# Values loaded as seven consecutive keys per partition, with the keys in the same order; scalings of q put off and turns of x moved

## The chip, the cores and the metric

The kernel runs on one core of one Trainium2 chip, as one launch. The metric is the device time of the launch in microseconds (us). Before the change three runs gave a median of 1261.9 us (1261.85 to 1263.39).

## The reference

Two blocks stand one after the other, all in float32. The first is attention with normalised queries and keys, for 8 batches of 12 heads, 448 positions and 64 channels; the second is an MLP mixer on the joined heads (768 channels).

```
q_n, k_n = rmsnorm(q, g_q), rmsnorm(k, g_k)             # over the 64 channels
attn = softmax(q_n @ k_n.T / sqrt(64))                  # over 448 keys
x = (attn @ v), heads side by side                      # 8 x 448 x 768
h = relu(x.T @ w_tok1) @ w_tok2                         # 448 -> 256 -> 448
u = x + h.T
out = u + relu(u @ w_ch1) @ w_ch2                       # 768 -> 1536 -> 768
```

The sum over the keys is the same in whatever order the keys are taken, as long as scores and values take the same one. That is what the change uses.

## The kernel before, in words

The work is written for heads in pairs: pair p holds two heads, there are 48 pairs, six to a batch, and two pairs are worked on together. The 448 keys of a head stand in NK = 7 blocks of 64. For each block the PE forms the scores with the keys as the stationary side (L475, into a PSUM tile s_ps), ACT takes their exponentials (L479, tile e), and the PE multiplies them with the values (L560, out to o_ps). The sums over the keys are made by matmuls with ones for the first pairs (L532) and by additions on DVE and POOL with one matmul for the later ones.

**How keys and queries come in.** `loads` (in class Pre, ending in L1625) fetches q and k of a pair. For pairs 0 to 11, called plain, q and k come by rows, and `turn_qk` turns them on the PE (L443, into t_ps); ACT then copies the keys out of PSUM (L453) and copies and scales the queries (L449). For pairs 12 to 47 q and k come in blocks of 32 by 32, four DMAs of 32 partitions for each, and DVE turns them (L446, one instruction for the keys of a pair and one for the queries, 72 in all). There the queries are scaled by ACT in place (L449) in a step of its own, `finish_q`. The scores of a pair wait for it; `score` calls it itself if it has not been called by then.

**How values come in.** `load_v` issues two DMAs for each pair on SP, one for each head (L417). A partition r holds the keys r, 64 + r, 128 + r and so on: seven runs of 64 floats (256 bytes) each. Three buffers (v_0, v_1, v_2, printed as v_69, v_70, v_71) take turns, and a load waits until the PE has used the values that were in its buffer. A SP DMA also waits for the completion of the one eight before it, as there are eight semaphores in rotation.

**The order of the work.** Each engine runs its instructions in the order in which the program issues them. A planner keeps a list of items with a cost in microseconds; `merge` lays lists between each other by these costs, and `later(us, fn)` puts a call off until the items issued since then have cost that much. `att_step(g)` gives the items of attention for the first 18 pairs (four steps to two pairs), `big_step` those of the later ones. Up to pair 19 the scaling is put off with `later(3.0, ...)` at L839.

**Turns of x.** In batch 0 the attention's output (tile uT) has to be turned for the token mixing. `trans_x` does it for 128 channels at a time: four PE transposes (L929, L931, into t_ps, the same PSUM banks as the scores), and three copies by ACT (L933 once, L935 twice). There are six such turns. `x_items(0, 0)` holds the first three and `x_items(0, 1)` the others; tok1 (L953, L960) is the first token matmul, which reads them.

**The first stage.** While batch 0 goes through its channel mixing (L1175 and on), the channel weights are still being converted from their form in DRAM: DMAs of raw (L231), then DVE (L354, L355, L357, L359, L388) and ACT (L365), chunk by chunk, in a chain that the matmuls of L1175 wait for. L1186 is a copy of ACT that frees one of their PSUM tiles. Later batches fetch the converted weights from DRAM (ws) by L1133, as tiles named unit.

Of the kernel before, what the change touches and what calls it, by code (L numbers as in the profile page):

```python
# [83 lines left out]
def whole(ctx, tc, shifted, pre, q, k, v, g_q, g_k, moe_w_tok1, moe_w_tok2, moe_w_ch1, moe_w_ch2, out):  # L84
# [328 lines left out]
    def load_v(p):  # L413
        b, hs = heads(p)
        st["v", p] = vt = pre.v_0 if p == 0 else st["v45"][:, p - 4, :] if p in (4, 5) else pre.v_t[p % 3]
        for a in range(2):
            nc.sync.dma_start(  # L417
                out=vt[rows_of(p, a)].rearrange("r (k d) -> r k d", d=D),
                in_=v[b, hs][a].rearrange("(k r) d -> r k d", r=D))

    def rows_of(p, a):

        return slice((a ^ p % 2) * D, (a ^ p % 2) * D + D)

    def scale(p):
        pre.scale(p, st)
# [6 lines left out]
    def turn_qk(p, i, apart=False):  # L433

        qk = st["qk", p]
        if ("qkT", p) not in st:
            st["qkT", p] = pre.qkT[p] if p < len(pre.qkT) else qkT_pool.tile([P, 2, S], F32, name="qkT")[:]
        to = st["qkT", p][:, i, :]
        if pre.plain(p):
            ps = s_tile("t_ps")  # L440
            for c in range(NS):
                o = (i * NS + c) * P
                nc.tensor.transpose(ps[:, c * R:(c + 1) * R], qk[0:R, o:o + P], ident[0:R, 0:R])  # L443
            src = ps[:, 0:S]
        else:
            nc.vector.transpose(out=to, in_=qk[:, i * S:(i + 1) * S])  # L446
            src = to
        if i == 0:
            st["mul", p] = lambda: nc.scalar.mul(to, src, g_t[:, 0:1])  # L449
            if not apart:  # L450
                finish_q(p)
        elif pre.plain(p):
            nc.scalar.copy(out=to, in_=src)  # L453
        if i == 0:
            st.pop(("qk", p))
# [297 lines left out]
    def att_step(g):  # L753
# [67 lines left out]
        if live and n < NP:  # L821
            late = n < 2 * NPAIR + 2
            if t >= NPAIR // 2 and late:
                if s == 1:
                    ahead, behind = f(pre.square, n), f(pre.reduce, n) + f(pre.square, n + 1)
                elif s == 2:
                    behind = f(pre.reduce, n + 1) + pre.roots(n, st) + scales(n)
                    if pre.plain(n):
                        sooner, behind = behind[:-2], [lambda: None] * len(behind[:-2]) + behind[-2:]
            elif t >= NPAIR // 2:  # L830
                a, b = f(pre.square, n) + f(pre.reduce, n), f(pre.square, n + 1) + f(pre.reduce, n + 1)
                behind = (a, b + pre.roots(n, st), scales(n), [])[s]
            now = {2: [] if pre.plain(n) else [n], 3: [n, n + 1] if pre.plain(n) else [n + 1]}.get(s, [])
            apart = not (shifted or pre.plain(n))

            def turn(q, i):
                turn_qk(q, i, apart)
                if apart and i == 0:
                    later(3.0, lambda: finish_q(q))  # L839
            turns = [lambda q=q, i=i: turn(q, i) for q in now for i in (1, 0)]  # L840

        inside = g < 2 * NPAIR
# [565 lines left out]
    AHEAD = 1  # L1408
# [36 lines left out]
    for part in pre.roots(2, st):  # L1445
        part()
    scale(2)
    scale(3)
    run(merge(
        att_items(1, 8) + merge(att_items(8, AHEAD * per + 1), x_items(0, 0)),  # L1450
        [(0.4, lambda: None)] + weight_items(0, BEFORE)))
    left, (some, sums) = [], sum_items()
    for b in range(B):
        early, double = middle_items(b)
        if b == 0:
            early, last = first_items(
                tok1_items(0, 0) + x_items(0, 1) + tok1_items(0, 1) + early, double, some)
        else:
            if b > 1 and in_next(b - 1):

                y, z = sends(b - 1, y_order(b - 1)[:4]), left
                left = [y[0], y[1], z[0], y[2], z[1], y[3]]
            run(merge(tok1_items(b, 0), left[:2]))
            begin, early = merge(tok1_items(b, 1) + early[:3 * KC], left[2:]), early[3 * KC:]
            if b == 1 and not shifted:
                run(merge(begin, sums[5:9]))
                early, begin = merge(early[:8], sums[9:]) + early[8:], []
            elif b == 1:
                early, begin = merge(begin + early[:8], sums[5:]) + early[8:], []
            if b == 1:  # L1470
                form_items()
            tail, keep = (4, 2) if b == 1 else (14, 3) if ending(b) else (11, 6)
            last, ends = double[-tail - keep:-tail], double[-tail:]
            double = double[:-tail - keep]
            early = begin + early + double
        lo = (b + AHEAD) * per + 1
        att = []
        if b + AHEAD < B and (shifted or b < 2):
            att = att_items(lo, lo + 10) + x_items(b + AHEAD, 0)
            if shifted:  # L1480
                att += att_items(lo + 10, lo + per)
            elif not b:
                step = att_step(lo + per - 1)
                att += att_items(lo + 10, lo + per - 1) + step[:5] + x_items(1, 1) + step[5:]
            else:
                run(att[:6])
                ahead, block, beside, between = big_step(BIG, False)
                att = att[6:] + att_items(lo + 10, lo + per - 1) + ahead + [block] + beside
                att += between[:6] + x_items(2, 1) + between[6:-3]
                behind_x = between[-3:]  # L1490
        elif b + AHEAD < B:
            t = (b + AHEAD) * NPAIR // 2
            blocks = [big_step(t + i // 2, i % 2) for i in range(1, NPAIR + 1)]
            blocks[4][3][10:10] = x_items(b + 1, 0)
            early = place(early, blocks, [near(early, at) for at in BLOCKS], in_seven(b))
        if b == 0:
            last = x_items(1, 1) * shifted + merge(last, sums[:5], turns(b, y_order(b)[2:4]))
        else:
            if b + 1 < B:
                last = merge(last, behind_x if b == 1 and not shifted else x_items(b + 1, 1))  # L1500
            if b == 2 and not shifted:
                last.append((0.4, right_sums))
            last += last_items(b, ends)
        run(merge(att, early) + last)
        if b == 0:
            load_units(0)
        left = [] if b and ending(b) else turns(b, y_order(b)[4:])
# [5 lines left out]
class Start:  # L1513
# [95 lines left out]
    def loads(self, p, st, eng, other):  # L1609
# [13 lines left out]
        def blocks(e, i, x, m):  # L1623
            o = 32 * m % D
            e.dma_start(  # L1625
                out=qk[32 * m:32 * m + 32, i * S:(i + 1) * S].rearrange("t (n c) -> t n c", c=32),
                in_=x[b, hs][32 * m // D][:, o:o + 32].rearrange("(n t) c -> t n c", t=32))

        fn, n = (plain, 2) if self.plain(p) else (blocks, 4)
        return [lambda e=e, i=i, x=x, m=m: fn(e, i, x, m)  # L1630
# [152 lines left out]
```

## Time and profile before

| | |
|---|---|
| median of three runs | 1261.9 us |
| the profiled execution: its time | 1260.77 us |
| the profiled execution: its span | 1259.0 us |
| granted TensorE clock, mean | 0.998 |
| PE busy | 1231.8 us, 98% |
| DVE, POOL, ACT busy | 871.6, 448.9, 418.9 us |

The time of the profiled execution holds 1.8 us that lie outside its span. The profile is one execution as the hardware profiler recorded it. Its page has the busy time of each engine, the span in 40 slices, the DMA queues, the chain of work that ended last, and groups of instructions. The trace behind it can be asked for one engine's instructions in a stretch of time (a timeline: start, length, engine, line, operation, tiles, count, and in brackets the idle time before it with what ended it), for all waits of one engine, for the busy time of every engine in given stretches, and for the time from a DMA's issue to its landing.

### The profile page before, as it was taken

How to read it: one execution, taken by the hardware profiler on the slowest of the kernel's cores; microseconds unless marked ns; L12 is line 12 of the kernel's file. 1: busy time of each engine (PE TensorE's matmuls, PEld its weight loads, DVE VectorE, ACT ScalarE, POOL GpSimd, SP SyncE). 2: the span in 40 equal slices, each digit the busy share in tenths (PEclk: the TensorE clock that was granted, in tenths of full speed). 3: DMA queues.
4: the chain of work that ended last, by engine and by line, in shares of the span. 5: the costliest groups of instructions: out<-in, count | busy, mean ns of one | idle time of the engine just before them, and what ended most of it. 6: DMA issues, size and time to landing. Idle time of an engine off the chain costs nothing.

```text
span 1259.0 us, 21357 instructions
## 1 busy us (share of the span) xinstructions
PE 1231.8 (98%) x7724; PEld 903.2 (72%) x7724; DVE 871.6 (69%) x1385; ACT 418.9 (33%) x896; POOL 448.9 (36%) x681
## 2 busy tenths in 40 slices
PE   6999998999999999999999999999999999999998
PEld 4444443457744488797778877897787877798998
DVE  6888899757774466877688486866768486656243
ACT  5764443224332144302442144312444034301210
POOL 2220650034996831334233232344132342133222
PEclk9999999999999999999999999999999999999999
DMA  8565797999899886794768667694777865487564
GB/s 199 120 169 157 214 256 194 207 250 251 228 246 208 199 203 167 159 244 93 178 166 216 158 152 177 152 238 102 188 169 161 214 129 155 120 201 175 167 175 105
DMA packets 480279, 228.46 MB, mean 181 GB/s; under 512 B 362900, under 2 KB 440084, under 8 KB 480164
## 3 DMA queue, kind: packets, MB, share of 16 engines
q1 hardware_dynamic: 472626, 211.85, 68.9%
q0 software_dynamic: 4512, 14.46, 3.9%
q8 instruction: 63, 1.03, 0.4%
q10 hardware_dynamic: 3026, 0.69, 0.3%
q14 instruction: 52, 0.43, 0.1%
HBM read 184.26 MB, written 42.66 MB: 180 GB/s over the span
## 4 chain that ended last, share of the span: by engine, by line
PE 78%; DVE 6%; DMA 1%; issue 1%; SPq 0%; ACT 0%; DVEq 0%; ACTq 0%
PE m_ps L1205 26%; PE m_ps L1271 22%; PE s_ps L475 8%; PE o_ps L560 8%; PE m_ps L1254 4%; PE t_ps L953 2%; PE m_ps L953 2%; PE seven_ps L1039 2%; PE m_ps L1039 1%; PE m_ps L1085 1%; DVE raw L357 1%; DVE raw L355 1%; PE m_ps L1175 1%; DVE stage L388 1%; DVE es L516 1%
## 5 line engine op out<-in xcount | busy, mean ns | idle before, releaser
L1271 PEld LDWEIGHTS m_ps<-hb,unit 128*128 128x128 f32 x1440 | 271.6, 190 | 7.4 <-issue 3.5
L1271 PE MATMUL m_ps<-hb,unit 128*128 128x224 f32 x1440 | 276.1, 353 | 0.2 <-ACT e L479 0.2
L1205 PE MATMUL m_ps<-tu,unit 128*128 128x224 f32 x1008 | 202.0, 355 | 2.0 <-DVE hb L1211 1.6
L1205 PEld LDWEIGHTS m_ps<-tu,unit 128*128 128x128 f32 x1008 | 189.0, 190 | 16.1 <-issue 7.8
L479 ACT ACTIVATE e<-s_ps 128x448 f32<-128x448 f32 x294 | 138.9, 548 | 122.4 <-PE s_ps L475 120.9
L475 PE MATMUL s_ps<-qkT 64*64 64x448 f32 (+1 forms) x1344 | 152.8, 545 | 1.2 <-ACT x L935 1.1
L1205 PE MATMUL m_ps<-uT,unit 128*128 128x224 f32 x756 | 151.1, 354 | 0.7 <-DVE hb L1211 0.6
L1205 PEld LDWEIGHTS m_ps<-uT,unit 128*128 128x128 f32 x756 | 142.2, 190 | 7.6 <-POOL tu L1109 3.1
L560 PE MATMUL o_ps<-e,v 64*64 64x448 f32 (+1 forms) x1288 | 136.5, 538 | 0.9 <-DMA v<-in_v_dram 0.7
L516 DVE TENSOR_TENSOR es<-es,e 128x896 f32<-128x896 f32 x90 | 101.3, 1126 | 8.7 <-ACT e L479 4.0
L1211 POOL TENSOR_TENSOR hb<-r,r 128x448 f32<-128x448 f32 x21 | 24.0, 1142 | 218.1 <-ACT r L1227 218.1
L475 PEld LDWEIGHTS s_ps<-qkT 64*64 64x64 f32 (+1 forms) x1344 | 46.9, 129 | 72.9 <-issue 51.2
L560 PEld LDWEIGHTS o_ps<-e,v 64*64 64x64 f32 (+1 forms) x1288 | 48.1, 127 | 61.0 <-issue 55.2
L1211 DVE TENSOR_TENSOR hb<-m_ps,r 128x448 f32<-128x448 f32 x63 | 38.9, 618 | 70.1 <-POOL r L1211 49.3
L1690 POOL TENSOR_TENSOR nt<-rs 128x56 f32<-128x56 f32 (+1 forms) x54 | 21.3, 394 | 180.3 <-DVE rs L1682 177.1
L1286 POOL TENSOR_TENSOR uT<-uT,r 128x448 f32<-128x448 f32 x42 | 54.6, 1315 | 77.9 <-DVE r L1286 50.5
L1212 ACT ACTIVATE hb<-hb 128x448 f32<-128x448 f32 x84 | 48.4, 576 | 101.3 <-DVE hb L1211 84.2
L1660 DVE TENSOR_REDUCE ms<-sq 128x28 f32<-128x896 f32 (+2 forms) x44 | 46.9, 1068 | 45.2 <-ACT sq L1647 38.7
L329 POOL TENSOR_TENSOR raw<-raw 128x128 f32<-128x128 f32 x128 | 68.2, 552 | 26.7 <-DMA raw<-wp 22.2
L1175 PE MATMUL m_ps<-hb,stage 128*128 128x448 f32 x144 | 57.4, 556 | 4.9 <-ACT r L1186 3.8
L1282 ACT COPY r<-m_ps 128x448 f32<-128x448 f32 x24 | 12.8, 532 | 140.2 <-PE m_ps L1271 140.2
L1711 DVE TENSOR_TENSOR qk_t<-qk_t,rs 128x896 f32<-128x896 f32 (+1 forms) x42 | 54.7, 1340 | 2.3 <-POOL rs L1693 2.3
(184 smaller groups left out, 1769.2 us busy)
## 6 DMA issues: line engine op xcount, KB each, us to landing
unit<-ws SPq DMA_DIRECT2D x267, 384.0 KB, 4.0
raw<-in_moe_w_ch_dram SPq DMA_DIRECT2D x72, 256.0 KB, 3.8
v<-in_v_dram SPq DMA_DIRECT2D x96, 112.0 KB, 3.9
out_dram<-turned SPq DMA_DIRECT2D x182, 56.0 KB, 2.0
xs<-xt SPq DMA_DIRECT2D x52, 168.0 KB, 4.1
qk_t<-in_q_dram SPq DMA_DIRECT2D x144, 56.0 KB, 3.5
qk_t<-in_k_dram SPq DMA_DIRECT2D x144, 56.0 KB, 3.7
x<-xs SPq DMA_DIRECT2D x39, 192.0 KB, 3.9
```

The lines of the kernel that those rows point to most:

```text
L329: nc.gpsimd.tensor_tensor(out=at[o], in0=at[x], in1=at[y], op=ALU.add if op == "+" else ALU.subtract)
L475: nc.tensor.matmul(out=pss[i][to:to + wide, 0:S], lhsT=qkT[h, 1, k * D + o:k * D + o + wide], rhs=qkT[h, 0, :], start=True, stop=True)
L479: nc.scalar.activation(out=e[:, i, :], in_=pss[i][:, 0:S], func=AF.Exp)
L516: nc.vector.tensor_tensor(out=es[:], in0=(es if k > 1 else st["e", t, 0])[:], in1=st["e", t, k][:], op=ALU.add)
L560: nc.tensor.matmul(out=st["o", p][o:o + wide, 0:S], lhsT=vt[rows, k * D + d:k * D + d + wide], rhs=e[rows, :], **kw)
L953: nc.tensor.matmul(out=st["t1", h][jc][:, 0:HC], lhsT=w1_sb[:, c, jc * P:(jc + 1) * P], rhs=st["x", b, h][:, :, c, :], start=start and c = ...
L1175: nc.tensor.matmul(out=ps, lhsT=a[:, o + 2 * half, :], rhs=natural(half * KF + t) if wide else u[:, half * KC + t, :], start=(t == 0 and h ...
L1205: nc.tensor.matmul(out=ps[:, j * HS:(j + 1) * HS], lhsT=w[:, t, j, :], rhs=m, start=(t == 0), stop=(t == KC - 1))
L1211: add = lambda e, o, x, y: e.tensor_tensor(out=o, in0=x, in1=y, op=ALU.add)
L1271: nc.tensor.matmul(out=ps[:, x * HS:(x + 1) * HS], lhsT=st["w"][:, tile_at % 6, :], rhs=hb[:, X_SLOT[f], i, :], start=(i == 0), stop=(i == 3))
L1286: e.tensor_tensor(out=get(out), in0=get(x_), in1=get(y), op=ALU.add if op == "+" else ALU.subtract)
L1711: self.nc.vector.tensor_tensor(out=part, in0=part, in1=r.unsqueeze(2).to_broadcast(list(part.shape)), op=ALU.mult)
```

## The change

It has four parts.

1. The values of a pair are loaded so that a partition holds seven consecutive keys, one run of 448 floats (1792 bytes). Plain pairs still take two DMAs of 64 partitions. The other pairs take four DMAs of 32 partitions, since there the 64 partitions of a block are two groups of 32 in another order of keys.
2. The keys are put in the same order: for plain pairs by the ACT copy out of PSUM, which now reads every seventh float; for the others by a k load that takes another order of rows, and by a DVE turn whose blocks are read and written in another order. The queries stay as they were.
3. The scaling of q is put off by 8.0 instead of 3.0 in the planner's microseconds. This concerns pairs 12 to 19.
4. Four of the six turns of x in batch 0, not three, lie among the attention steps ahead of its last one; that last step stands by itself behind them. The other two turns follow with the token mixing.

```diff
@@ load_v
         for a in range(2):
-            nc.sync.dma_start(
-                out=vt[rows_of(p, a)].rearrange("r (k d) -> r k d", d=D),
-                in_=v[b, hs][a].rearrange("(k r) d -> r k d", r=D))
+            to, src = vt[rows_of(p, a)], v[b, hs][a]
+            if pre.plain(p):
+                nc.sync.dma_start(out=to, in_=src.rearrange("(r k) d -> r (k d)", r=D))
+                continue
+            src = src.rearrange("(t m k) d -> m t (k d)", m=2, k=NK)
+            for m in range(2):
+                nc.sync.dma_start(out=to[32 * m:32 * m + 32], in_=src[m])
@@ turn_qk
             src = ps[:, 0:S]
+            if i:
+                src = src.rearrange("p (r k) -> p k r", k=NK)
+                to = to.rearrange("p (k r) -> p k r", k=NK)
         else:
-            nc.vector.transpose(out=to, in_=qk[:, i * S:(i + 1) * S])
+            src = qk[:, i * S:(i + 1) * S]
+            if i:
+                nc.vector.transpose(
+                    out=to.rearrange("p (k m c) -> p m k c", m=2, c=32),
+                    in_=src.rearrange("p (m k c) -> p m k c", m=2, c=32))
+            else:
+                nc.vector.transpose(out=to, in_=src)
@@ att_step
-                    later(3.0, lambda: finish_q(q))
+                    later(8.0, lambda: finish_q(q))
@@ the call of the first steps
+    first_x = x_items(0, 0) + x_items(0, 1)
     run(merge(
-        att_items(1, 8) + merge(att_items(8, AHEAD * per + 1), x_items(0, 0)),
+        att_items(1, 8) + merge(att_items(8, AHEAD * per), first_x[:KC + 1]) + att_items(AHEAD * per, AHEAD * per + 1),
         [(0.4, lambda: None)] + weight_items(0, BEFORE)))
...
-                tok1_items(0, 0) + x_items(0, 1) + tok1_items(0, 1) + early, double, some)
+                tok1_items(0, 0) + first_x[KC + 1:] + tok1_items(0, 1) + early, double, some)
@@ blocks, in loads
-                in_=x[b, hs][32 * m // D][:, o:o + 32].rearrange("(n t) c -> t n c", t=32))
+                in_=x[b, hs][32 * m // D][:, o:o + 32].rearrange("(t n) c -> t n c" if i else "(n t) c -> t n c", t=32))
```

The numbers of lines grow by 13 in most of the program (L475 becomes L488, L449 becomes L462, L1186 becomes L1199).

On ACT, at pair 12 (about 194 to 210 us of the trace before), these rows stood one behind the other; L449 is the scaling, L479 the exponentials, L365 a step of the weight conversion, r the copy of L1186:

```order
L449 ACTIVATE qkT<-qkT,g_t 128x448
L479 ACTIVATE e<-s_ps 128x448 x4
L365 ACTIVATE raw<-raw,expo_c 128x512 x2
L1186 COPY r_19297<-m_ps 128x448
L1186 COPY r_19302<-m_ps 128x448
```

In the change the same place reads:

```order
L492 ACTIVATE e<-s_ps 128x448 x4
L365 ACTIVATE raw<-raw,expo_c 128x512
L462 ACTIVATE qkT<-qkT,g_t 128x448
L365 ACTIVATE raw<-raw,expo_c 128x512
L1199 COPY r_19371<-m_ps 128x448
L1199 COPY r_19376<-m_ps 128x448
```

The scaling of pair 12 has moved behind the four exponentials and one conversion step, and stays ahead of the two copies.

On PE, at the end of batch 0's attention (about 70 to 82 us), with t_ps and uT the turns of x, L953 and L960 tok1, L475 the scores:

```order
L475 MATMUL s_ps<-qkT 64x448 x4
L929 MATMUL t_ps<-ident,uT 128x128 x3
L931 MATMUL t_ps<-ident,uT 64x128
L953 MATMUL m_ps<-x,w_sb 128x384 x3
L960 MATMUL m_ps<-x,w_sb 128x384 x2
L475 MATMUL s_ps<-qkT 64x448 x8
```

In the change:

```order
L488 MATMUL s_ps<-qkT 64x448 x4
L966 MATMUL m_ps<-x,w_sb 128x384 x3
L973 MATMUL m_ps<-x,w_sb 128x384 x2
L488 MATMUL s_ps<-qkT 64x448 x8
```

The third turn is gone from the place right ahead of tok1: it stands some 20 rows earlier, and the fourth a few rows behind it, among the scores and values of pairs 4 and 5. Behind the second part of tok1 two turns follow each other where there were three.

On SP, in a batch of the later part (at about 758 us of the trace before), the loads of values for two pairs and the weight tiles beside them:

```order
L1133 DMA unit<-ws_17246 128x768 x5
L417 DMA v_71<-in_v_dram 64x7x64 x2
L417 DMA v_69<-in_v_dram 64x7x64 x2
L1133 DMA unit<-ws_17246 128x768 x2
```

In the change:

```order
L1146 DMA unit<-ws_17318 128x768 x5
L423 DMA v_71<-in_v_dram 32x448 x4
L423 DMA v_69<-in_v_dram 32x448 x4
L1146 DMA unit<-ws_17318 128x768 x2
```

The values of two pairs take eight issues on SP where they took four, and the weight tiles behind them follow four issues later.

## The prediction

> **What bounds the kernel now.** I read the page first, then all waits of PE, then the chain, then timelines at the few places where PE stands still. The page:
>
> ```profile
> PE 1231.8 (98%) x7724; PEld 903.2 (72%) x7724; DVE 871.6 (69%) x1385; ACT 418.9 (33%) x896; POOL 448.9 (36%) x681
> PE 78%; DVE 6%; DMA 1%; issue 1%; SPq 0%; ACT 0%; DVEq 0%; ACTq 0%
> ```
>
> PE is busy for 1231.8 of 1259.0 us, and the chain is PE for 78% of the span. No matmul is removed here; the change can only win what PE loses in waits. All waits of PE:
>
> ```profile
> PE first_ps L163 <- DVE ms L1660: 10.3, 1, 10.3
> PE m_ps L1175 <- ACT r L1186: 3.8, 2, 3.3
> PE m_ps L1205 <- DVE hb L1211: 2.2, 2, 1.6
> PE s_ps L475 <- ACT x L935: 1.1, 2, 0.8
> PE m_ps L953 <- ACT x L933: 0.9, 1, 0.9
> PE s_ps L475 <- ACT e L479: 0.9, 1, 0.9
> ...
> PE o_ps L560 <- DMA v<-in_v_dram: 0.7, 1, 0.7
> ```
>
> Without the start's 10.3 us and the 2.2 us on L1211, which the change doesn't touch, there are 3.8 + 1.1 + 0.9 + 0.9 + 0.7 = 7.4 us for it to win. Whether a wait counts depends on its place, so next the chain between 150 and 272 us (start, length, what):
>
> ```profile
> 223.43 3.35 DMA raw<-in_moe_w_ch_dram
> ...
> 241.47 0.97 DVE ms L1660
> 243.09 9.29 PE m_ps L1175 x24
> ```
>
> From about 161 us to 243.09 the pieces of the chain are nearly all DVE's conversions of the channel weights; ahead of that and from 243.09 on it is PE. So a wait of PE between these two points is worth nothing by itself: PE meets the conversion chain at 243.09 anyway. A wait ahead of it counts, if DVE waits for PE there. DVE at 154 us and the stretches of 200 to 243 us (length, then busy time of PE, PEld, DVE, ACT, POOL, granted clock, DMA share, GB/s):
>
> ```profile
> 154.22 0.71 DVE L621 STREAM_TRANSPOSE dt<-d_ps 128x224 f32<-128x224 f32 x2 [2.93 <-PE d_ps L532]
> 200.00:220.00 20.00, 16.73 (x72) 7.26 (x70) 19.56 (x33) 7.24 (x13) 2.25 (x2) 0.91 0.75 184
> 220.00:243.00 23.00, 21.70 (x64) 10.47 (x56) 21.18 (x41) 7.31 (x15) 2.24 (x2) 1.00 0.96 221
> ```
>
> DVE stood 2.93 us for PE's sums, so up to that much of what PE wins ahead of 154 us is passed on to the chain.
>
> **Turns of x.** PE, then ACT, from 73 to 85 us:
>
> ```profile
> 73.00 2.20 PE L953 MATMUL m_ps<-x,w_sb 128*128 128x384 f32 x6 [0.91 <-ACT x L933]
> 83.58 2.47 PE L475 MATMUL s_ps<-qkT 64*64 64x448 f32 x10 [0.77 <-ACT x L935]
> ...
> 83.55 0.48 ACT L933 COPY x<-t_ps 128x384 f32<-128x384 f32 x1
> 83.93 0.54 ACT L935 COPY x<-t_ps 64x128 f32<-64x128 f32 x2
> 84.49 0.48 ACT L933 COPY x<-t_ps 128x384 f32<-128x384 f32 x1
> ```
>
> The first wait is tok1's for the third turn's copies. That turn now stands well ahead, so 0.91 us goes. The second is the scores' for PSUM banks that three turns in a row hold; one turn costs ACT 84.49 - 83.55 = 0.94 us, and with two turns instead of three the banks come free about that much earlier: 0.9 us, the wait of 0.77 and a little of the spread-out scores behind it. Together 1.8 us. The transposes are the same in number. What it costs: two more sets of copies (2 x 0.94 us on ACT) now lie among the exponentials of pairs 4 and 5, where ACT has pauses. If they hide, 0; if each delays the exponentials in full, 1.9 us, and the gain is gone. I take 0.6, a third, since ACT is busy for two thirds of 40 to 100 us:
>
> ```profile
> 40.00:100.00 60.00, 56.90 (x738) 26.56 (x719) 50.53 (x85) 40.73 (x92) 12.64 (x25) 1.00 0.48 134
> ```
>
> Gain 1.2 us (-0.1 to 1.8).
>
> **Loads at the start.** Everything arrives under load in the first 40 us, and PE then misses exponentials:
>
> ```profile
> 0.00:40.00 40.00, 29.42 (x526) 16.75 (x534) 28.31 (x63) 24.82 (x47) 12.97 (x35) 1.00 0.91 196
> 42.47 0.96 PE L475 MATMUL s_ps<-hb 64*32 64x448 f32 x8 [0.87 <-ACT e L479]
> ```
>
> With the DMA engines busy for 0.91 of that time and v in runs seven times longer, the loads ahead of those exponentials should land somewhat sooner. Between 0 and 0.87 us; I take 0.5.
>
> Against it stands the copy of the keys out of PSUM, now with a stride of 28 bytes. The rows for that copy and, as the only strided read near it, for two reciprocals on DVE (the second strided, in SBUF):
>
> ```profile
> L453 ACT COPY qkT<-t_ps 128x448 f32<-128x448 f32 x9 | 5.1, 566 | 1.8 <-PE t_ps L443 1.8
> ...
> L607 DVE RECIPROCAL v_first<-v_first 128x28 f32<-128x28 f32 x18 | 5.9, 328 | 0.6
> L626 DVE RECIPROCAL v_first<-dt 64x28 f32<-64x28 f32 x6 | 1.9, 320 | 0.2
> ```
>
> There the stride costs nothing (320 against 328 ns). Two such copies stand on the way to the first scores; if each took twice as long, that would be 2 x 0.57 = 1.1 us. The other ten lie beside PE's work for earlier pairs. Between 0 and 1.1 us; I take 0.2, nearer to the strided row. [...]
>
> **Turns of keys on DVE.** 36 of the 72 turns read and write in another block order:
>
> ```profile
> L446 DVE STREAM_TRANSPOSE qkT<-qk_t 128x448 f32<-128x448 f32 x72 | 41.8, 616 | 2.9 <-PE s_ps L475 2.9
> ```
>
> The rows inside a block stay contiguous, the elements the same; I take 0. If they took twice as long, only the two that lie in DVE's chain (pairs 12 and 13) would count, 2 x 0.62 = 1.2 us. Later DVE has pauses: it is busy 69% of the span.
>
> **The scaling put off.** ACT, then PE, at pair 12:
>
> ```profile
> 205.09 0.67 ACT L449 ACTIVATE qkT<-qkT,g_t 128x448 f32<-128x448 f32 x1 [10.09 <-DVE qkT L446]
> 205.66 1.82 ACT L479 ACTIVATE e<-s_ps 128x448 f32<-128x448 f32 x4
> 207.36 1.42 ACT L365 ACTIVATE raw<-raw,expo_c 128x512 uint32<-128x512 uint32 x2
> 208.65 0.99 ACT L1186 COPY r<-m_ps 128x448 f32<-128x448 f32 x2
> ...
> 209.26 3.20 PE L1175 MATMUL m_ps<-hb,stage 128*128 128x448 f32 x4 [3.27 <-ACT r L1186]
> ```
>
> ACT stood 10.09 us for DVE's turn with the exponentials behind it, PE missed the copy of L1186 for 3.27 us, and then ran at a lower clock: 0.91 on average between 200 and 220 us; four matmuls took 3.20 us. In the change the exponentials and one conversion go ahead of the scaling, so L1186 starts about 205.09 + 0.67 + 0.71 - 0.2 = 206.3 us instead of 208.65, and PE waits about 1 us. But this is inside the stretch where the chain is DVE's: PE, 3 to 5 us sooner, stands for conversions behind it. I take 0 (0 to 1.0). The later scalings move behind other steps of ACT (pair 19's behind copies that wait for DVE), with work of PE for other pairs ahead of the scores; 0, at most 0.5.
>
> **Values in later batches.** SP issues 72 more DMAs. Where do loads of v end just in time? There is the one wait of 0.7 us at 348.90, and in each later batch a place where two pairs' values are loaded shortly ahead of their use, here at 612 us (SP's issues, their median time to landing, PE's first uses of the two tiles):
>
> ```profile
> 612.17 2.63 SPq L417 DMA_DIRECT2D v<-in_v_dram  x4
> ...
> v<-in_v_dram SPq DMA_DIRECT2D x4, 112.0 KB, 3.5
> ...
> 618.29 0.91 PE L560 MATMUL o_ps<-e,v 64*64 64x448 f32 x4
> 618.67 0.54 PE L560 MATMUL o_ps<-cv_sb,v 64*64 64x448 f32 x2
> ```
>
> An issue takes 2.63 / 4 = 0.66 us, so the last begins at 614.2, lands at about 617.7, and is used at 618.67: 1 us to spare. Such places are in five batches. Now eight issues. What do they cost? Rows of issue times and of landings:
>
> ```profile
> L417 SPq DMA_DIRECT2D v<-in_v_dram x96: 595/622/2177, 10.4 to 1078.1; - x96
> L1133 SPq DMA_DIRECT2D unit<-ws x267: 319/345/3420, 265.0 to 1235.3; - x134
> ...
> v<-in_v_dram SPq DMA_DIRECT2D x96, 112.0 KB, 3.9
> out_dram<-turned SPq DMA_DIRECT2D x182, 56.0 KB, 2.0
> ```
>
> A weight tile has one run for each of 128 partitions and is issued in 345 ns; a new v load has one run for each of 32 partitions. By that row the last of eight begins at 7 x 0.39 = 2.7 us behind the first, against 2.0 before: 0.7 us later. It carries 56 KB, and a DMA of that size lands in 2.0 instead of 3.9 us; under the load here I count on 0.7 to 1.5 us sooner. So nothing is late: 0. At the old issue time the last would begin 7 x 0.66 - 2.0 = 2.6 us later, which is a rival below. The wait at 348.90 may shrink or grow: I take a gain of 0.2 (-0.7 to 0.7).
>
> The Trainium skill has a rule against cutting loads up: "SBUF — State Buffer", section "The DMA setup-cost knee", counts about 2 us for every transfer, whatever its bytes, plus bytes at 436 GB/s. By it half the bytes land only 0.13 us sooner (an estimate from that page), 0.6 us of the later issue would be left, and the spare 1 us above would still cover it. The 3.9 and 2.0 us of the rows differ by far more than its term for bytes.
>
> **The sum.** -1.2 (turns of x) - 0.5 (start) + 0.2 (strided copies) + 0 (turns of keys) + 0 (scaling) - 0.2 (values) = -1.7 us, against the profiled execution's 1260.77 (its span of 1259.0 and 1.8 outside it): 1259.1. The median of the runs, 1261.9, lies 1.1 higher; for it the sum gives 1260.2. With the terms at their ends the gain lies between 1.8 + 0.9 + 1.0 + 0.7 = 4.4 and, on the other side, a loss of 0.1 + 1.1 + 1.2 + 0.5 + 0.7 = 3.6; hardly all at one end.
>
> **The rivals.**
>
> *The stall at 206 us counts in full.* If DVE's chain follows ACT's steps, so that the conversions come sooner as well, the 2.3 us of ACT, the clock lost there and the wait itself are kept: 3.3 + 1.8 = 5.1 us. The clock's part is 20.00 x 0.09 = 1.8 us. For it: the conversions of L365 are ACT's, and two of them stood behind the scaling. Against it: DVE was busy for 19.56 of the 20 us. Time 1260.2 - 5.1 = 1255.1. Chance 0.12.
>
> *Nothing arrives at the end.* The DMA share is 0.96 between 220 and 243 us, and 3.35 us of the chain is a load of raw. If the loads, not DVE, set the pace there, what PE wins ahead of 154 us is lost at 223. Time 1261.7. Chance 0.26.
>
> *The eight issues make the second pair's values late.* If an issue of a v load costs 0.6 us whatever its shape, the last begins 2.6 us later. If it then lands 0 to 1.5 us sooner, it is 2.6 to 1.1 us late against 1 us to spare: 0.1 to 1.6 us of wait, in five batches 0.5 to 8 us, in the middle 4.2. It decides from 1 us of lateness on. For it: 72 instructions of 0.6 us and the rows above. Against it: the weight tile's 345 ns. Time 1260.2 + 4.2 = 1264.4, slower. Chance 0.16.
>
> *The small gains as summed*: 0.46.
>
> **The numbers.** The likeliest is the sum, 1260.2. About 0.2%, 2.5 us, is what a measurement of this kernel can tell from no change. Faster by more: the first rival's 0.12 and 0.4 of the 0.46 for the sum (terms towards their good ends), 0.18: 0.30. Slower: the third rival's 0.16 and 0.02 from the strided copies: 0.18. The rest, 0.52, is within. The range 1256.0 to 1264.5 takes in the sum's own terms, the second rival and the nearer half of the third; it leaves out most of the first and the far half of the third, some 0.18.
>
> **What would show it.** In the profile of the changed kernel: the wait of L953 (now L966) on ACT gone; the scores' wait on L935 (now L948) under half; the copy of keys at about 0.57 us; the turns of keys at 0.62 us; the wait on r of 3.3 us gone or near 1 us, the clock at 1.00 between 200 and 220 us, and PE waiting instead for DVE's stage ahead of 243; v's issues near 0.35 us and no wait of L560 (now L573) for v at the five places. The forecast is wrong if the first channel matmul behind DVE's chain starts 4 us sooner (first rival), if it starts as late as before (second), or if PE waits for v in each batch (third).

## The result, and the profile after

The changed kernel takes 1270.0 us (median of four runs, 1267.89 to 1271.62) against 1262.14 us before (four runs). The ratio is 1.0062, with a 95% interval of 1.0045 to 1.0079: slower by 5.7 to 10.0 us, where 1.7 us faster was forecast. The profiled execution took 1267.89 us, with a span of 1266.1.

The page after, busy times and the chain that ended last:

```profile
PE 1233.7 (97%) x7724; PEld 913.6 (72%) x7724; DVE 867.5 (69%) x1385; ACT 419.3 (33%) x896; POOL 452.2 (36%) x681
...
PE 80%; DVE 7%; DMA 5%; SPq 3%; issue 2%; ACT 2%; POOL 1%; DVEq 0%; ACTq 0%; POOLq 0%
```

PE does the same work (1233.7 against 1231.8 us); it stands longer. In the chain, DMA has gone from 1% to 5% and SP's queue from nothing to 3%. The waits of PE after that bear on the change:

```profile
...
PE m_ps L1218 <- DVE hb L1224: 3.5, 3, 1.5
PE s_ps L488 <- ACT x L948: 3.5, 3, 1.8
PE m_ps L1188 <- ACT r L1199: 3.0, 1, 3.0
PE o_ps L573 <- DMA v<-in_v_dram: 1.8, 1, 1.8
PE m_ps L1098 <- DVE uT L1103: 1.7, 2, 1.4
PE m_ps L1267 <- DVE uT L1272: 1.7, 1, 1.7
```

The wait of tok1 for a copy of x (0.9 us) is gone, as forecast. The scores' wait for the copies has gone from 1.1 to 3.5 us instead of halving. The wait on hb (L1211 before, L1224 now), which the prediction set aside as untouched, has gone from 2.2 to 3.5 us. The waits on DVE for uT, 0.3 us before, are 1.7 us at each of two lines. The 3.0 us on r are a wait at 231 us; the one of 3.3 us at 206 us is gone.

Setting each matmul of the token and channel mixing against the same one before gives where the time went. At 101 us (the second token matmul, L1085 before) the changed kernel is 1.9 us behind, at 243 us 1.5, at 327 us 3.4, at 350 us 4.3, at 384 us 5.0, at 407 us 6.8, and it stays 6.5 to 7.2 behind to the end. So there are two places: ahead of 110 us, and 300 to 415 us. Between them the conversion chain gives a little back.

One caution for everything below. In one set of comparisons 31 runs of the kernel before spread from 1257.46 to 1266.77 us. A single profile can be several us off; the ratios, in the experiments from 4 to 12 runs of a kernel against 11 to 35 of before, carry the sizes, and the profiles show the mechanism. A ratio is turned into us with 1262.

### The profile page after: what moved, and what is told of

Same layout as the page of the kernel before. It is cut to its first block, busy times and chain, and to the rows that moved or that the text cites. A ratio compares the mean times of both kernels' runs of the same rounds, so it can differ in the third digit from the quotient of the medians.

```text
span 1266.1 us, 21463 instructions
## 1 busy us (share of the span) xinstructions
PE 1233.7 (97%) x7724; PEld 913.6 (72%) x7724; DVE 867.5 (69%) x1385; ACT 419.3 (33%) x896; POOL 452.2 (36%) x681
## 3 DMA queue, kind: packets, MB, share of 16 engines
q8 instruction: 63, 1.03, 0.3%
## 4 chain that ended last, share of the span: by engine, by line
PE 80%; DVE 7%; DMA 5%; SPq 3%; issue 2%; ACT 2%; POOL 1%; DVEq 0%; ACTq 0%; POOLq 0%
PE m_ps L1218 24%; PE m_ps L1284 20%; PE s_ps L488 9%; PE o_ps L573 8%; PE m_ps L1188 5%; PE m_ps L966 2%; PE t_ps L966 2%; PE seven_ps L1052 2%; PE m_ps L1098 2%; PE m_ps L1267 1%; SPq L1639 1%; PE m_ps L1052 1%; DMA unit<-ws 1%; DMA xs<-xt 1%; DMA v<-in_v_dram 1%
## 5 line engine op out<-in xcount | busy, mean ns | idle before, releaser
L488 PE MATMUL s_ps<-qkT 64*64 64x448 f32 (+1 forms) x1344 | 153.6, 548 | 3.5 <-ACT x L948 3.5
L1224 POOL TENSOR_TENSOR hb<-r,r 128x448 f32<-128x448 f32 x21 | 24.2, 1151 | 218.8 <-ACT r L1240 218.8
L488 PEld LDWEIGHTS s_ps<-qkT 64*64 64x64 f32 (+1 forms) x1344 | 50.0, 129 | 72.1 <-issue 49.0
L573 PEld LDWEIGHTS o_ps<-e,v 64*64 64x64 f32 (+1 forms) x1288 | 52.9, 127 | 56.1 <-issue 49.9
L1224 DVE TENSOR_TENSOR hb<-m_ps,r 128x448 f32<-128x448 f32 x63 | 38.9, 619 | 73.5 <-POOL r L1224 52.7
L329 POOL TENSOR_TENSOR raw<-raw 128x128 f32<-128x128 f32 x128 | 66.8, 541 | 26.5 <-DMA v<-in_v_dram 19.9
L1267 PE MATMUL m_ps<-hb,unit 128*128 128x448 f32 x144 | 55.5, 543 | 1.7 <-DVE uT L1272 1.7
```

The lines of the kernel that those rows point to most:

```text
L329: nc.gpsimd.tensor_tensor(out=at[o], in0=at[x], in1=at[y], op=ALU.add if op == "+" else ALU.subtract)
L488: nc.tensor.matmul(out=pss[i][to:to + wide, 0:S], lhsT=qkT[h, 1, k * D + o:k * D + o + wide], rhs=qkT[h, 0, :], start=True, stop=True)
L573: nc.tensor.matmul(out=st["o", p][o:o + wide, 0:S], lhsT=vt[rows, k * D + d:k * D + d + wide], rhs=e[rows, :], **kw)
L1224: add = lambda e, o, x, y: e.tensor_tensor(out=o, in0=x, in1=y, op=ALU.add)
L1267: nc.tensor.matmul(out=ps, lhsT=w[:, t, :], rhs=natural(half * KF + t), start=(half == 0 and t == 0), stop=(half == 1 and t == KF - 1))
```

## The parts by themselves

Theory A: two costs add up, the turns of x ahead of 110 us, and behind 300 us SP's queue, whose issues (the time SP spends on handing over a DMA) have become more and dearer. Theory B: only the early loss is real and shifts the rest.

**Turns of x alone.**

```diff
+    first_x = x_items(0, 0) + x_items(0, 1)
...
-        att_items(1, 8) + merge(att_items(8, AHEAD * per + 1), x_items(0, 0)),
+        att_items(1, 8) + merge(att_items(8, AHEAD * per), first_x[:KC + 1]) + att_items(AHEAD * per, AHEAD * per + 1),
...
-                tok1_items(0, 0) + x_items(0, 1) + tok1_items(0, 1) + early, double, some)
+                tok1_items(0, 0) + first_x[KC + 1:] + tok1_items(0, 1) + early, double, some)
```

> Before, with the turns of x moved and nothing else. Theory A (two costs that add up: the turns of x cost about 1.5 us of what the whole change lost by 243 us, SP's dearer issues the 5 us behind 300): 1.5 to 3 us slower than before, with PE waiting on the copies of x near 54 and 84 us for 2.5 to 3.5 us, and no wait for v at 351. Theory B (the early loss shifts everything behind it and the loads of values cost nothing by themselves): 6 to 8 us slower.

Measured: ratio 1.0011 (0.9997 to 1.0025), 1.4 us slower, not told apart from nothing with certainty. The waits near 56, 84 and 101 us are those of the changed kernel.

**The scaling alone.**

```diff
-                    later(3.0, lambda: finish_q(q))
+                    later(8.0, lambda: finish_q(q))
```

> Before, with the scaling put off by 8.0 and nothing else. Both theories: within 0.5 us of before; the stall of 3.3 us at 206 us is gone, and PE waits for conversions ahead of 243 us instead; the matmul that started at 243.09 starts within 0.5 us of that.

Measured: 0.9994 (0.9981 to 1.0007), no change that can be told from nothing. PE from 203 to 246 us, with what it waited for in brackets:

```profile
206.04 6.28 PE L1175 MATMUL m_ps<-hb,stage 128*128 128x448 f32 x16 [0.40 <-ACT r L1186]
...
232.15 9.29 PE L1175 MATMUL m_ps<-hb,stage 128*128 128x448 f32 x24 [2.76 <-ACT r L1186]
242.28 4.03 PE L1175 MATMUL m_ps<-hb,stage 128*128 128x448 f32 x10 [0.84 <-DVE stage L388]
```

The stall of 3.27 us has become 0.40, and 2.76 us stand at 232 us instead of 0.57 before. The matmul of 243.09 starts at 242.28, in a run that was 0.7 us ahead at its first matmul already (9.6 against 10.3). What PE won it gave back: the copies of r at 232 us stand behind DVE's work on ACT, and DVE is no sooner. The granted clock between 200 and 220 us is 1.00 here, against 0.91 before.

**Values and keys alone** (parts 1 and 2 of the change, the rest as before).

> Before, with values and keys in the new order and nothing else. Theory A: 4 to 6 us slower, nearly all of it between 300 and 415 us, with a wait for v near 350 us and q and k landing several us later near 400 us. Theory B: within 1 us of before.

Measured: 1.0053 (1.0034 to 1.0072), 6.7 us slower. That is nearly the whole loss, and theory B falls.

**The plain pairs alone**: their two loads with long runs and the strided copy of their keys.

```diff
+            if pre.plain(p):
+                nc.sync.dma_start(out=to, in_=src.rearrange("(r k) d -> r (k d)", r=D))
+                continue
...
+            if i:
+                src = src.rearrange("p (r k) -> p k r", k=NK)
+                to = to.rearrange("p (k r) -> p k r", k=NK)
```

> Before, with the new order for the plain pairs alone (two DMAs with long runs, the strided copy of keys), the other 36 pairs as before. Theory A: within 1 us of before, rather faster (0 to 0.9 us), as no issue on SP is added. Theory B: the same. If the strided copy or the landing order at the start cost something, it shows here as a loss ahead of 100 us.

Measured: 1.0000 (0.9984 to 1.0017). No loss, and no gain that can be told. So the 6.7 us belong to the 36 later pairs.

## What in the values and keys

The later pairs' loads differ in three ways: four issues of v instead of two, longer runs, and k in another order of rows. Issues on SP (ns: shortest, median, longest), of k before, of k after, of v after:

```profile
L1625 SPq DMA_DIRECT2D qk_t<-in_k_dram x144: 332/477/2462, 153.4 to 1037.4; - x144
```

```profile
L1639 SPq DMA_DIRECT2D qk_t<-in_k_dram x144: 560/621/2420, 155.7 to 1047.2; - x144
```

```profile
L423 SPq DMA_DIRECT2D v<-in_v_dram x148: 310/420/1562, 180.8 to 1085.9; - x148
```

An issue of v went from 622 to 420 ns, but there are four where two stood: 4 x 0.42 - 2 x 0.62 = 0.44 us more for a pair. An issue of k went from 477 to 621 ns, with the same shape, bytes and number: 4 x 0.144 = 0.58 us more. By these medians SP is busy for 1.0 us longer for each pair, and two pairs follow each other.

The first place where this reaches PE is 306 to 327 us. POOL's part of the weight conversion (L329) before and after, then DVE after:

```profile
314.61 3.83 POOL L329 TENSOR_TENSOR raw<-raw 128x128 f32<-128x128 f32 x8 [17.72 <-DMA raw<-wp]
```

```profile
318.51 5.41 POOL L329 TENSOR_TENSOR raw<-raw 128x128 f32<-128x128 f32 x8 [19.93 <-DMA v<-in_v_dram]
```

```profile
326.13 0.62 DVE L1224 TENSOR_TENSOR hb<-m_ps,r 128x448 f32<-128x448 f32 x1 [3.47 <-POOL r L1224]
```

The loads of raw that L329 needs stand behind v, q and k on SP. The first is issued at 311.73 instead of 308.66 us and the last lands at 318.37 instead of 314.49, just ahead of L329 (the row after names v, but L329 reads raw). PE is 1.5 us late there; raw is 3 to 4 us late. POOL's part of hb follows L329, DVE waits 3.47 us for POOL, and PE waits for DVE's hb. This wait of PE is 2.9 to 4.4 us in the five profiles with k's new order and at least two loads of v for each pair, and 1.6 to 2.2 in all the others.

**Four loads, runs as before.**

```diff
+            to, src = vt[rows_of(p, a)], v[b, hs][a].rearrange("(k r) d -> r k d", r=D)
+            for r in (0,) if pre.plain(p) else (0, 32):
+                n = D if pre.plain(p) else 32
+                nc.sync.dma_start(out=to[r:r + n].rearrange("r (k d) -> r k d", d=D), in_=src[r:r + n])
```

> Before, with the values of the 36 later pairs fetched by four DMAs of 32 partitions with the old runs of 256 bytes, the old order of keys. Theory A1 (the number of issues on SP costs the time): 3 to 6 us slower, as with the values' change. Theory A2 (the k loads in the new order of rows cost it, 0.62 us for each issue instead of 0.48): within 1 us of before.

Measured: 1.0022 (1.0004 to 1.0039), 2.8 us slower (0.5 to 4.9).

**Two loads with long runs.**

```diff
+            nc.sync.dma_start(out=vt[rows_of(p, a)], in_=v[b, hs][a].rearrange("(r k) d -> r (k d)", r=D))
```

> Before, with the values of all pairs by two DMAs with runs of 1792 bytes, and the keys left in their old order, so that scores and values no longer belong together and the output is not the reference's. It tells what the long runs are worth without more issues. Both theories: 0 to 3 us faster, if landings at 348 us and at the start matter; the loads of values land sooner than 3.9 us after issue.

Measured: 0.9983 (0.9971 to 0.9995), 2.1 us faster. The long runs look worth something, as the change's first part has it, so long as they take no more issues.

**The k loads' order alone.**

```diff
-                in_=x[b, hs][32 * m // D][:, o:o + 32].rearrange("(n t) c -> t n c", t=32))
+                in_=x[b, hs][32 * m // D][:, o:o + 32].rearrange("(t n) c -> t n c" if i else "(n t) c -> t n c", t=32))
```

> Before, with the k loads of the later 36 pairs in the new order of rows and nothing else, so that keys and values no longer belong together and the output is not the reference's. Theory A1: within 1 us of before. Theory A2: 3 to 6 us slower, with issues of k at 0.58 to 0.62 us instead of 0.48 and SP later by some 0.5 us for each pair.

Measured: 1.0023 (1.0011 to 1.0036), 2.9 us slower. A1 and A2 were put as alternatives; each accounts for a part.

**Four loads with long runs.** As two long loads, but in pieces of 32 partitions.

> Before, with the values by four DMAs of 32 partitions with runs of 1792 bytes, the keys left in the old order, so that the output is not the reference's. Against four short loads it tells the worth of the long runs, against two long loads (2.1 us faster than before) that of two issues more. If issues count: 2 to 3 us slower than two long loads, so 0 to 1 us slower than before. If not: 2 us faster than before.

Measured: 1.0020 (1.0008 to 1.0032), 2.5 us slower, against 2.1 us faster with two: 4.6 us between them (2.5 to 6.8 by their intervals), more than twice the long runs' gain. With the 2.9 us of k's order this makes 5.4 of the 6.7 us (whose interval is 4.3 to 9.1).

**Values and keys as in the change, but two loads.** If DVE's turn writes column 2t + m instead of 32m + t, a partition holds seven consecutive keys in plain order, and one DMA of 64 partitions loads them.

```diff
-                    out=to.rearrange("p (k m c) -> p m k c", m=2, c=32),
+                    out=to.rearrange("p (k c m) -> p m k c", m=2, c=32),
```

> Values and keys in the new order, no other part of the change, but the later pairs' values by two DMAs of 64 partitions: DVE's turn of the keys writes every second column, so that a partition holds seven consecutive keys in plain order. If the two extra issues of a pair cost 2 to 3 us, it is that much faster than the values and keys of the change by themselves (6.3 us slower than before), so 3 to 4 us slower than before, the rest being the k loads' dearer issue. If the turn with a stride is dear, L459 shows it.

Measured: 1.0017 (1.0004 to 1.0030), 2.1 us slower, against 6.7 with four loads: 4.6 us here too (1.6 to 7.4). DVE's turn with every second column takes 639 ns against 600 for the plain one of the queries:

```profile
L450 DVE STREAM_TRANSPOSE qkT<-qk_t 128x448 f32<-128x448 f32 x36 | 23.0, 639 | 2.3 <-PE s_ps L483 2.3
```

**k and q in the dear order.**

```diff
+                in_=x[b, hs][32 * m // D][:, o:o + 32].rearrange("(t n) c -> t n c", t=32))
```

> Before, with the k loads and the q loads of the later 36 pairs in the new order of rows, so that the output is not the reference's. If the dearer issue of such a load (0.62 instead of 0.48 us) on SP's queue is what k's new order costs (2.9 us for 144 loads), 288 of them cost about twice that: 5 to 6 us slower than before. If the cost lies in the keys alone, 3 us.

Measured: 1.0073 (1.0048 to 1.0098), 9.2 us slower (6.1 to 12.4), about three times the 2.9 of k alone and more than was expected. Twice as many dear issues, at least twice the loss. Here the path can be read, because the wait comes in every batch. All waits of PE on POOL, then the chain around 555 us:

```profile
PE m_ps L1271 <- POOL hb L1245: 4.8, 4, 1.9
```

```profile
540.53 0.96 ACT sq L1647
...
545.30 1.00 POOL nt L1690
...
550.78 3.45 POOL uT L1286 x3
554.23 2.19 POOL hb L1245
...
556.47 3.67 PE m_ps L1271 x18
```

ACT takes the squares of the next q and k as soon as they have landed. Behind that, in order, come DVE's sums, POOL's iterations for the root, and only then POOL's part of the MLP (hb), for which PE waits. Four waits, 4.8 us in all; the list of before has none on POOL. ACT's squares wait 4.75 us for k there, against 3.63 before. PE feels it 16 us further on, through ACT, DVE and POOL.

In the changed kernel a like path, by way of DVE, closes at 413 us. The chain from 384 us on:

```profile
384.43 10.85 DMA xs<-xt
...
398.92 1.92 SPq L1639
400.88 2.28 SPq L1639
403.21 2.42 SPq L1639
...
406.37 2.69 DMA qk_t<-in_k_dram
...
409.17 0.96 ACT sq L1661
...
412.76 0.54 DVE uT L1272
413.34 1.77 PE m_ps L1267 x4
```

The last five issues of k and q take 0.62 to 2.42 us here, behind the transfers of the turned x; in the kernel before they took 0.48 to 1.91. The wait for the DMA eight before is not what holds them: for the issues at 400.88 and 403.21 us that one had landed at 395.71 and 395.98. What holds them these runs don't show. The waits of ACT's squares for k, summed over the run, before and after (us in total, times, longest):

```profile
ACT sq L1647 <- DMA qk_t<-in_k_dram: 37.6, 12, 14.9
```

```profile
ACT sq L1661 <- DMA qk_t<-in_k_dram: 48.6, 14, 18.8
```

**Tiny DMAs.** To load SP's queue without moving bytes:

```diff
+    pad = dram.tile([P, D], F32, name="pad")
...
+            if not pre.plain(p):
+                o = 2 * p + a
+                nc.sync.dma_start(out=pad[o:o + 1], in_=v[b, hs][a][0:1])
```

> Before, with 72 more DMAs on SP, one behind each load of values of the 36 later pairs, each moving 256 bytes within DRAM to a place that nobody reads. If the number of issues in SP's queue costs the time (each takes its issue and a place in the rotation of eight), 2 to 3 us slower, as the four short loads were (2.8). If the shape of the loads cost it, within 0.5 us of before.

Measured: 1.0203 (1.0183 to 1.0223), 25.6 us slower. It did not test what it was meant to. These DMAs depend on nothing, and though the program has them behind the loads of v they stand in SP's queue between 60 and 115 us, ahead of the loads that matter there:

```profile
60.03 16.85 SPq L423 DMA_DIRECT2D pad<-in_v_dram  x19
```

```profile
105.25 1.06 ACT L1648 ACTIVATE sq<-qk_t 112x1024 f32<-112x1024 f32 x1 [27.86 <-DMA qk_t<-in_k_dram]
```

Nineteen DMAs of 256 bytes held SP for 16.85 us, 0.9 us each. ACT stood 27.86 us for q and k behind them, and PE 22.1 us. It shows how much SP's place in line is worth, not what the change's issues cost.

**One load for every second pair.** Values and keys with two loads, as above, but for even pairs both heads by one DMA of 128 partitions; and the same with the scaling put off:

```diff
+        if p % 2 == 0:
+            nc.sync.dma_start(out=vt, in_=v[b, hs].rearrange("a (r k) d -> (a r) (k d)", r=D))
+            return
```

> As values_two (values and keys in the new order, two loads for a pair), but the values of every second pair come by one DMA of 128 partitions, so that a pair takes 1.5 issues on average. If the time goes with the number of SP's issues (four: 6.3 us slower than before, two: 2.2), this is another 1 us faster: 1 to 1.5 us slower than before. If only the fourfold load is bad, 2.2 us slower as values_two.

> values_one with the scaling put off by 8.0 as in the change. The scaling by itself measured 0.8 us faster than before, within what can be told from nothing: 0 to 1 us faster than values_one, level with before or slower by up to 1.5 us.

Measured: 1.0127 (1.0111 to 1.0144) and 1.0110 (1.0094 to 1.0127): 16 and 14 us slower, against all expectation. In the profile of the first nearly all of it is one wait:

```profile
PE m_ps L1265 <- DVE uT L1270: 10.6, 1, 10.6
```

What SP did ahead of it, its waits and its issues:

```profile
SPq L313 <- DMA ws<-raw: 16.5, 2, 11.1
```

```profile
381.81 0.93 SPq L313 DMA_DIRECT2D raw<-wp  x2
382.84 0.45 SPq L1144 DMA_DIRECT2D unit<-wp  x1
383.37 1.95 SPq L1636 DMA_DIRECT2D qk_t<-in_q_dram  x4
```

```profile
391.26 14.86 DMA xs<-xt
```

SP stood for 11.1 us, up to 381.81, in front of two loads of raw, until a store from their buffer (ws<-raw) had landed. In the kernel before, these two loads stand behind q, k and the turned x, at 407.44 us, and q goes out at 371.16; here it goes out at 383.37, and the turned x 13 us later than before. Its last transfer then took 14.86 us, against 8.75 (378.04 to 386.79); why was not tried. The edit does not touch the loads of raw: what moved them ahead is the order in which the build put SP's DMAs. The second kernel has the same order, and SP stands at the same loads until 383.87. By these two profiles the 16 and 14 us come from two loads in a bad place, and say nothing of the price of an issue; that order without the other edits was not run.

**The order in SP's queue.** This holds for other versions too. The description of the kernel before, by which each engine runs its instructions in the order in which the program issues them, does not fit SP: an edit that changes only the shape or number of v's loads leaves other DMAs in other places. Set one by one against the kernel before, SP's DMAs stand in the same order with k's order alone, with k and q in the dear order, and with the scaling alone. With four long loads, with values and keys alone and with the plain pairs alone, a few have moved between 158 and 171 us, in the changed kernel some also at 101 to 111; the plain pairs' 1.0000 says that the former cost nothing that can be told. With two long loads, a load of k, a weight tile and two loads of v have moved at 371 to 403 us as well, and with four short loads there are such places in every batch. So the 2.9 and 9.2 us of the dear order, and the 2.5 us of four long loads against before, are prices in a queue of nearly the same order. The 4.6 us of four loads against two hold a change of order too, and how much of them it is was not tried.

## What in the turns of x

PE in the changed kernel at the three waits, then PE before ahead of the second, then ACT in the changed kernel at the first:

```profile
56.35 0.97 PE L488 MATMUL s_ps<-qkT 64*32 64x448 f32 x4 [1.83 <-ACT x L948]
...
82.97 0.98 PE L488 MATMUL s_ps<-qkT 64*64 64x448 f32 x8
85.20 1.53 PE L488 MATMUL s_ps<-qkT 64*64 64x448 f32 x6 [1.25 <-ACT x L948]
...
103.02 1.39 PE L1098 MATMUL m_ps<-w_sb,h 128*128 128x448 f32 x3 [1.43 <-DVE uT L1103]
```

```profile
81.84 0.97 PE L475 MATMUL s_ps<-qkT 64*64 64x448 f32 x4
```

```profile
52.98 0.53 ACT L948 COPY x<-t_ps 64x128 f32<-64x128 f32 x2
53.54 0.97 ACT L671 COPY uT<-o_ps 128x448 f32<-128x448 f32 x2
54.52 0.84 ACT L647 COPY v_first<-v_first 32x14 f32<-32x14 f32 x4
55.38 0.48 ACT L946 COPY x<-t_ps 128x384 f32<-128x384 f32 x1
```

At 52 us two turns follow each other on PE, and ACT has 1.8 us of other copies between their copies; the second turn keeps its bank that long. At 84 us there are two turns instead of three. The wait itself is longer (1.25 against 0.77 us), but ahead of it eight scores are done where four were in the same time, and those behind follow closer: from 73 to 88 us the changed kernel makes up 0.88 us on the one before, half of it (0.44) the third turn's work on PE, which now stands earlier. So of the two places the first loses, and it loses by what stands between the copies on ACT.

**Four turns, spread.** The turns among all five steps, the last one too, so that no two follow each other ahead of tok1.

```diff
+    first_x = x_items(0, 0) + x_items(0, 1)
...
+        att_items(1, 8) + merge(att_items(8, AHEAD * per + 1), first_x[:KC + 1]),
```

> Before, with four turns of x ahead of tok1 as in the change, but laid among all five attention steps, the last one too, so that the first two turns do not follow each other. Theory X1 (two turns back to back keep the scores from their PSUM banks, with other ACT work between their copies): the wait near 54 us is under 0.7 us, tok1 waits for nothing, 0.5 to 2 us faster than the version with the turns moved as in the change. Theory X2 (four turns ahead of tok1 are one too many wherever they lie): as that version, 1 to 2 us slower than before.

Measured: 1.0015 (1.0003 to 1.0027), 1.9 us slower. The wait near 54 us is down to 0.31 us as X1 has it, tok1 waits for nothing, but 0.61 us stand at 60 us, 1.26 at 84 and 1.75 at 102, and the time is not better. X1 names one wait rightly; the time is as X2 has it.

**The merge held.** At 101 us PE before had turns of q and k (L443) between the second token matmuls. With one item less in the list the merge lays them further on. An empty item puts them back:

```diff
+                tok1_items(0, 0) + [(0.1, lambda: None)] + first_x[KC + 1:] + tok1_items(0, 1) + early, double, some)
```

> Before, with the turns of x moved as in the change, and an empty item left in the list of the first stage in place of the turn that went, so that the merge lays the PE's turns of q and k between the second token matmuls again, as before. If the wait of 1.4 us near 101 us comes from those turns having moved, it is gone here and the kernel is 1 to 1.5 us faster than with the turns alone (1.4 us slower than before), about level with before. If it comes from the moved turns of x themselves, it stays, and so does the time.

Measured: 1.0037 (1.0020 to 1.0055), 4.7 us slower. The turns of q and k stand between the matmuls again, and still 1.03 us are waited there. So the wait comes mostly from elsewhere: DVE reaches the sums for uT at 102.35 us in the changed kernel, behind conversion steps, where it began them at 100.11 before (the steps between its sums are the same 4.5 us; it starts late as a whole, on POOL's rs, at 96.69 instead of 94.41):

```profile
102.35 1.14 DVE L1103 TENSOR_TENSOR uT<-uT,m_ps 128x448 f32<-128x448 f32 x2
```

```profile
100.11 0.61 DVE L1090 TENSOR_TENSOR uT<-uT,m_ps 128x448 f32<-128x448 f32 x1
```

Why this version is slower than the turns alone stays open; the waits in its profile don't show it.

## Why the prediction was wrong, point by point

- **Values in later batches**: the step that failed. It asked whether v itself would be late at the five places where two pairs are loaded, and there it was right. SP and PE at such a place in the changed kernel:

```profile
764.30 3.67 SPq L423 DMA_DIRECT2D v<-in_v_dram  x8
768.06 0.84 SPq L1146 DMA_DIRECT2D unit<-ws  x2
```

```profile
770.49 0.83 PE L573 MATMUL o_ps<-cv_sb,v 64*64 64x448 f32 x4
```

  PE's values follow the first issue by 6.2 us, as before, without a wait. The third rival, v late in each batch, did not happen. SP does not even fall behind there: eight issues take 3.67 us instead of four in 2.63, but the next load of k goes out 7.38 us after the first of them in both kernels, and from 413 us on PE loses almost nothing more. What the step left out is what stands behind v in the queue where SP has no such pause, at 300 to 415 us: raw, q, k and the turned x feed paths through ACT, DVE and POOL that had no time to spare. The sum had no term for them, and it took the 2.2 us on L1211 as untouched, which became 3.5. The one wait for v, forecast to gain 0.2 us, went from 0.7 to 1.8 us; but it is 2.2 us with the turns of x alone as well, so one profile decides nothing there. Of the step's sizes, an issue was taken at 345 ns by the weight tile's row, and the row measured is 420. A load of 56 KB was to land 0.7 to 1.5 us sooner, by the row of a store; it lands in 3.2 instead of 3.9 us, the near end. The loads of q and k, of the same size, had 3.5 and 3.7 us in the profile before. The count of new DMAs is 74, not 72 (148 loads of v for 74).
- **Turns of keys**: DVE's part was right (634 ns where written in another order, 601 for the queries). But part 2 of the change has a DMA as well, and the prediction gave the k load no cost at all. Its issue is 144 ns dearer, and the new order by itself costs 2.9 us. A step that moves data counts with its DMA: here the missing term was the load's new order of rows, not the turn.
- **The scaling put off**: right in mechanism and size. The stall at 206 us went, PE stood at 232 us instead, for copies that stand behind DVE's work, and the time did not change (0.9994, 0.9981 to 1.0007). The first rival, worth 5.1 us, is out.
- **Strided copies**: right, and better than taken. The copy of the keys with its stride of 28 bytes takes 563 ns, against 566 without:

```profile
L466 ACT COPY qkT<-t_ps 128x448 f32<-128x448 f32 x9 | 5.1, 563 | 5.0 <-PE t_ps L447 5.0
```

  The Trainium skill says in "SBUF — State Buffer", section "Door 1: The DMA port swizzle", that access to PSUM that is not contiguous slows matmuls significantly. This copy is a read by ACT, and nothing of the kind shows in it.
- **Loads at the start**: the wait of 0.87 us at 42 us is gone in the profiles with the plain pairs' long runs, as forecast; that it is worth 0.5 us can't be told, as the plain pairs alone measure 1.0000 (0.9984 to 1.0017).
- **Turns of x**: a gain of 1.2 us was forecast, and 1.4 us slower (-0.4 to 3.2) was measured. The two gains came much as forecast: tok1's 0.9 us, and 0.88 us by 88 us, part of it only work that has moved. What failed is the cost. It was taken as 0.6 us, as if ACT's pauses hid two of three parts; the scores wait 0.43 and 1.83 us at 53 and 56 us, against 0.35 before, so 1.9 us, the upper end. And DVE's sums for uT, which make PE wait 1.43 us at 103 us, have no term in the sum.

The parts by themselves, 6.7 + 1.4 - 0.8, make 7.3 us, against the whole change's 5.7 to 10.0. The rule of the Trainium skill on cutting up loads ("SBUF — State Buffer", section "The DMA setup-cost knee") was weighed for the time of one transfer alone, which is what its sum counts. Here each smaller load landed sooner, and the kernel was slower; what stands behind the loads in the queue is not in that sum.

## What to carry to other kernels

When a change alters DMAs, cost the queue that issues them: number times issue time, then name the next few DMAs behind them and the last engine that waits for those, however far along. Compare the order of the queue in the two builds first: an edit of one load can move others. An order of rows that leaves bytes and shape alone can still make each issue dearer, so a reordered load needs its own row. And a wait for a PSUM bank is read from what the copying engine does between the copies, not only from how many copies there are.

## What the runs showed of the hardware that was not expected

- The issue of the k load, with the same 56 KB and the same runs of 128 bytes, takes 621 instead of 477 ns when its runs come from consecutive rows for a partition; the loads landed no later (3.2 against 3.7 us from issue).
- The granted clock fell after some gaps of PE and not after others, and not by their length. The stretch of 352 to 358 us in the kernel with values and keys alone, behind a gap of 1.62 us, and 229 to 239 us with the scaling alone, in which the gap of 2.76 us lies:

```profile
352.00:358.00 6.00, 6.00 (x12) 2.68 (x11) 2.46 (x3) 1.39 (x4) 5.75 (x9) 0.72 0.93 248
```

```profile
229.00:239.00 10.00, 7.24 (x20) 3.52 (x19) 9.67 (x21) 4.69 (x10) 2.24 (x2) 1.00 0.92 204
```

  What else decides it these runs don't show.
